# Attention, then two mixtures of experts, on one core: a transpose moved by a chunk, low parts of W1 moved between engines, the second lead's rows turned in one tile

## The chip, the cores and the metric

The kernel runs on one core of a Trainium2 chip. Its time is the device time of one execution in microseconds (us). A profiled execution has in addition a span, from the first to the last instruction that the trace shows. PE is the matmul engine (PEld its weight load), DVE the vector engine, ACT the scalar engine, POOL is GpSimd, and SP issues most DMAs.

## The reference

Three stages follow each other. The first is a linear attention over 2 batches, 8 heads, 768 positions and head size 48, with a decayed state. The second is a mixture of eight experts that gives each of the 1,536 rows to its best expert. The third is such a mixture again, with a capacity for each expert.

```python
# attention, for every position t
cur = einsum(u * k_t, v_t)
y_t = r_t @ (state + cur)
state = w * state + einsum(k_t, v_t)

# first mixture (second: no bias, and rows past an expert's capacity give 0)
logits = x @ w_gate + modality_bias[modality_id]
e_idx = argmax(logits); gate_w = softmax(logits)[e_idx]
for e in range(8):
    h = maximum(x[e_idx == e] @ w1[e], 0.0)      # 384 -> 1024
    out[e_idx == e] = gate_w * (h @ w2[e])       # 1024 -> 384
```

All is float32 outside. Where the kernel wants more than one float32r product gives, it splits a matrix into a high part (a cast) and a low part (the matrix less its cast), and multiplies high by high, low by high and high by low.

## The kernel before, in words

**Attention** goes through 12 chunks of 128 positions (the loop `for i in range(n)`, `n = 12`). In each chunk PE makes the scores (L262), DVE masks them (`am`, L266) and decays keys and queries of the next chunk (L233, L234), PE sums values (L283), and DVE adds POOL's diagonal term `av` (L250) in L288, the chunk's output. POOL's `av` of a chunk needs eight sums that ACT makes (L246), and these need POOL's two products (L240, L241) of the same chunk. Beside the chunks the kernel routes rows for the first mixture: gate logits (L319, L322), a choice (L368 to L376), lists, and from chunk 7 on the expert with most rows is known, the **lead**. Its 256 first rows are gathered to `XB0` (L707) in chunk 10, and its weights are split: `ex.high` on ACT (L677), `ex.low` on DVE or on POOL (L685), in pieces of 128x512, W1 having six.

`ids()` (L1081 to L1084) turns the rows' modality numbers, a 12x128 tile, into a column for each chunk: a DVE cast, a PE transpose, a DVE copy out of PSUM. `biases()` makes the bias of each row from it on POOL (L1088 to L1091), for L322 of chunk 0, which is done in chunk 1 or 2.

**The mixtures.** `Experts.two` does the lead's 256 rows. Its matmuls (L785) are interleaved with the routing of the other rows (hooks by number). Then tiles of 128 rows follow (`tile_a(u)`), each of one expert. A tile is done in a normal form with split weights (`tile1`, L758 up, L806 down), or in a small one (`tile3`, L868, L883, L896). A tile has points at which other work is hooked in: "begin", "first", "turn", "logits", "down", "half", "last". In the run that is profiled the first mixture has tiles 1 to 13; tile 9 is small, tile 10 is normal, tiles 11 to 13 are small. Splitting of the next tile's W1 is in `split1` (L689 a cast on ACT, L690 a subtraction on DVE, in three pieces of 128x1024), and stands under a condition on a number that is read from a table.

For the second mixture a **second lead** is chosen in tile 8 (`PICK`), and its weights are loaded to the same place as the first lead's (`R[0]`, `r0a` and `r0b` in the trace). Its rows are gathered again to `XB0`. From tile 9 on (`SURE - 1`), its rows are turned: `flip` transposes 128 rows on PE (L722, three transposes), and `parts0` makes their high part on ACT (L734) and their low part on DVE (L735). Half 0 is at the "last" point of tile 9, half 1 at that of tile 10. At the "last" point of tile 9 ACT and DVE also read two numbers, `when` and `behind` (`read_when`): in the tile whose number is `when`, ACT and DVE split the second lead's W1. It is 10 in this run. The second `two` starts at 252.08 us.

The order of instructions on each engine is that in which the code is written; nothing is rescheduled. An engine takes its instructions in order and waits at one whose inputs are not there.

Of the kernel before, what the change touches and what calls it, by code (L numbers as in the profile page):

```python
# [18 lines left out]
EN = mybir.EngineType  # L19
# [6 lines left out]
B, H, S, HD = 2, 8, 768, 48  # L26
D = H * HD
# [4 lines left out]
NT = NTOK // P  # L32
# [15 lines left out]
SURE = NTOK // P - 2  # L48
# [541 lines left out]
class Experts:  # L590
# [327 lines left out]

    def read_when(self):

        self.when, self.behind = self.words(3, 2, [EN.Activation, EN.DVE])

    def exit_hint(self, u):

# [115 lines left out]
def program(tc, r, k, v, w, u, mod, wg1, bias, w1a, w2a, wg2, w1b, w2b, cap, out):  # L1040
    nc = tc.nc
    with (
# [9 lines left out]
        banks = [pp.tile([P, 512], F32, name=f"bank{i}") for i in range(8)]  # L1052
# [3 lines left out]
        with tc.tile_pool(name="att", bufs=1) as ap:  # L1056
            ex = Experts(tc, K, wp, mp, banks)
            bs = ap.tile([P, 2, E], F32, name="bs")
            md = ap.tile([NT, P], I64, name="md")
            cpi = ap.tile([P, 1], I64, name="cpi")  # L1060
            wg2s = cp.tile([P, KD, 32], F32, name="wg2s")
            ra = Router(tc, K, mp, banks[7], None, "ra")
            ex.begin(w1a, w2a, x0, x1, ra, wg2s)
            capf = cp.tile([P, 1], F32, name="capf")

            def small():
                nc.sync.dma_start(
                    bs.rearrange("p m e -> p (m e)"),
                    bias.rearrange("m e -> (m e)").unsqueeze(0).to_broadcast([P, 2 * E]),
                )  # L1070
                nc.sync.dma_start(md, mod.rearrange("(c p) -> c p", p=P))

            def small2():
                with nc.allow_non_contiguous_dma(reason="one number a partition"):
                    nc.sync.dma_start(cpi, cap.unsqueeze(0).to_broadcast([P, 1]))
                nc.vector.memset(wg2s, 0.0)
                nc.sync.dma_start(wg2s[:, :, 0:E], wg2.rearrange("(q p) e -> p q e", p=P))

            mdf, mf, b2 = ap.tile([NT, P], F32, name="mdf"), ap.tile([P, NT], F32, name="mf"), ap.tile(TE, F32, name="b2")

            def ids():  # L1081
                nc.vector.tensor_copy(mdf, md.bitcast(I32).rearrange("c (p o) -> c p o", o=2)[:, :, 0])
                nc.tensor.transpose(banks[7][:, 0:NT], mdf, K.ident[0:NT, 0:NT])
                nc.vector.tensor_copy(mf, banks[7][:, 0:NT])  # L1084

            def biases():
                V = nc.gpsimd
                V.tensor_mul(b2, bs[:, 1:2].to_broadcast(TE), mf.unsqueeze(2).to_broadcast(TE))  # L1088
                V.tensor_scalar(mf, mf, -1.0, 1.0, op0=ALU.mult, op1=ALU.add)
                V.tensor_mul(bt, bs[:, 0:1].to_broadcast(TE), mf.unsqueeze(2).to_broadcast(TE))  # L1090
                V.tensor_add(bt, bt, b2)  # L1091

            n = len(ORDER)
            K.begin(nc, ap)
            rows = [xb[:, 0] for xb in ex.XB] + [ex.OB0[:, h] for h in range(2)]
            xts = [ex.xt[:, i] for i in range(2)]
            at = Attention(tc, cp, ap, mp, K, banks, rows, xts, r, k, v, w, u, wg1, bt, x0)
            small()
            for i in range(2, at.NB):
                at.load(i)  # L1100
            small2()
            ex.zero()
            ra.zero()
            at.flip(0)
            at.pnT_()
            at.warm(4)
            at.bonus1(0)
            at.natural_powers()
            at.bonus2()
            at.decayed(0)  # L1110
            for i in range(n):
                more = i + 1 < n
                at.scores(i)
                if more:
                    at.flip(i + 1)
                if i > 0:
                    at.route1(i - 1)
                at.bonus3(i)
                if more:
                    at.bonus1(i + 1)  # L1120
                if more:
                    at.decayed(i + 1)
                if i == 3:
                    nc.gpsimd.tensor_copy(capf, cpi.bitcast(I32)[:, 0:1])
                if i == EARLY + 1:
                    ra.count(0, EARLY)
                if i == EARLY + 4:
                    ra.list0(EARLY)
                    ex.gather(0, ex.XB0, rows=EARLY * P)
                if i == n - 1:  # L1130
                    ex.high(ex.R[0], 5)
                    ex.low(ex.R[0], 4)
                    ex.low(ex.R[0], 1, 3, 5, eng=EN.Pool)
                at.outs(i)
                if i == 0:
                    ids()
                    biases()
                if more:
                    at.bonus2()
                if i > 0:  # L1140
                    at.route2(i - 1)
                if i == EARLY + 4:
                    ex.low(ex.R[0], 0, 2)
                if i + at.NB < n:
                    at.load(i + at.NB)
                if i == EARLY:
                    ra.choose(at.L, 0, EARLY)
                if i == EARLY + 1:
                    ra.lead()
                    ex.load(ex.R[0], w1a, w2a, ra.fe[0:1, 0:1])  # L1150
                    ra.select1(EARLY)
                if i == EARLY + 2:
                    ra.select2(EARLY)
                if i == EARLY + 3:
                    ra.rows(EARLY)
                    ex.high(ex.R[0], 0, 2, 4)
                if i == EARLY + 4:
                    ra.spent(EARLY)
                    ex.high(ex.R[0], 1, 3)
                if i == 2:  # L1160
                    K.more(nc, cp)
                if i == 3:
                    K.more2(nc, cp)
            px = [banks[2][:, 0:D], banks[3][:, 0:D]]
            for h in range(2):
                ex.flip(ex.XB0, h, px[h])
            for h in range(2):
                ex.parts0(h, px[h])
            at.route1(n - 1)
        with tc.tile_pool(name="moeb", bufs=1) as mb:  # L1170
# [103 lines left out]
            def tile_a(u):  # L1274

                H = {p: [] for p in ("begin", "first", "turn", "logits", "down", "half", "last")}
# [31 lines left out]

                if u == PICK:
                    H["last"].insert(0, b3)  # L1310
                if u in (SURE - 1, SURE):
                    h = u - SURE + 1
                    H["last"] += [lambda: ex.flip(ex.XB0, h), lambda: ex.parts0(h)]
                if u == SURE - 1:
                    H["last"].append(ex.read_when)
                H["down3"] = [(lambda p: lambda: part2(p))(p) for p in range(2) if u > SURE + p]
# [5 lines left out]
                def split1():  # L1322
                    if u < U:
                        with tc.If(ex.split(u + 1)):
                            ex.split1(ex.slot(u + 1))
                    if u >= SURE:
                        with tc.If(ex.when == u):
                            ex.split1(ex.R[0])

                nothing = lambda: None  # L1330
                nxt = (
                    (lambda: ex.flip(xb(u + 1))) if u < U else nothing,
                    ex.parts if u < U else nothing,
                    split1,
                )
                if SURE <= u < U:
# [22 lines left out]
            def tile_b(u):  # L1359
# [16 lines left out]
                {-1: [a0, a1], 0: [a2], 2: [a3], 8: [ra.plan2], 10: [a4], 18: [ex.read, first_tile], 22: [ra.early]}  # L1376
            )
            tile_a(1)

            ex.begin(w1b, w2b, x1, out, rb)  # L1380
# [48 lines left out]
```

## Time and profile before

| | us |
|---|---|
| median of 3 runs | 377.67 |
| lowest, highest | 376.71, 382.09 |
| the profiled execution | 377.47 |
| its span in the trace | 375.8 |
| outside of the span | 1.7 |

PE is busy for 330.5 us of the span, DVE for 232.0, ACT for 156.0, POOL for 134.8. The matmul clock granted is 0.961 of the full one on average. Attention fills the span up to about 75 us, the first `two` from there to about 97 us, tiles 1 to 8 to 194 us, tile 9 to 205 us, tile 10 to 222 us, tiles 11 to 13 to 249 us, and the second mixture the rest.

### The profile page before, as it was taken

What the parts mean: (1) busy time and instruction counts of PE and PEld (TensorE: products, weight loads), DVE (VectorE), ACT (ScalarE), POOL (GpSimd) and SP (SyncE); (2) the same over time, 40 slices, a digit from 0 to 9 for tenths busy, and PEclk for the clock granted to TensorE, in tenths of its full rate; (3) what the DMA queues carried; (4) which work ended last, traced back from release to release, by engine and by line L of the source; (5) the groups of instructions that cost most, each with busy time, mean ns of one, the idle gap of its engine ahead of it and who ended that gap; (6) DMA issues with size and microseconds to landing.
All of it is one profiled execution on the core that took longest, in us unless ns stands there. A gap on an engine that the chain in (4) does not pass through costs nothing. (4 is left out here: it accounts for less than half of the span.)

```text
span 375.8 us, 9045 instructions
## 1 busy us (share of the span) xinstructions
PE 330.5 (88%) x2888; PEld 271.1 (72%) x2888; DVE 232.0 (62%) x675; ACT 156.0 (42%) x500; POOL 134.8 (36%) x165
## 2 busy tenths in 40 slices
PE   7699999969999999999995969869997989998960
PEld 6699988859878888888873844449886877574430
DVE  5679899979853444444657776645838395753330
ACT  3577566725042233333215644423146263823220
POOL 7888876935503222111214222311522212232230
PEclk9899999958999999999999898999999999999995
DMA  7858679452262111029899990000189998999400
GB/s 141 152 121 182 151 159 330 156 210 91 59 231 96 46 44 34 34 60 371 323 406 394 335 334 24 11 19 3 44 298 390 340 346 294 391 347 393 161 14 13
DMA packets 69509, 70.94 MB, mean 189 GB/s; under 512 B 41542, under 2 KB 61744, under 8 KB 69416
## 3 DMA queue, kind: packets, MB, share of 16 engines
q1 hardware_dynamic: 65704, 61.69, 50.0%
q0 software_dynamic: 3712, 8.18, 6.6%
q8 instruction: 38, 0.62, 0.7%
q14 instruction: 55, 0.45, 0.4%
HBM read 60.73 MB, written 12.55 MB: 195 GB/s over the span
## 5 line engine op out<-in xcount | busy, mean ns | idle before, releaser
L714 POOL DMA_INDIRECT x<-ob,raidx x14 | 15.3, 1095 | 104.8 <-DVE sn L845 57.9
L774 DVE TENSOR_TENSOR hl<-bank,hh 128x512 fp32r<-128x512 f32 x28 | 19.1, 689 | 39.8 <-ACT hh L773 38.5
L763 ACT ACTIVATE hs<-bank 128x512 f32<-128x512 f32 x28 | 16.7, 598 | 54.7 <-PE bank L758 46.7
L758 PE MATMUL bank<-w1l,xh 128*128 128x512 f32 x84 | 34.1, 407 | 3.3 <-DVE g L747 3.1
L714 POOL DMA_INDIRECT out<-ob,rbidx x12 | 12.1, 1006 | 69.2 <-DVE ex L742 57.1
L806 PE MATMUL bank<-w2h,hh 128*128 128x384 f32 x144 | 35.0, 353 | 0.0
L758 PE MATMUL bank<-w1h,xh 128*128 128x512 f32 x84 | 34.1, 407 | 0.0
L758 PE MATMUL bank<-w1h,xl 128*128 128x512 f32 x84 | 33.9, 403 | 0.0
L806 PE MATMUL bank<-w2l,hh 128*128 128x384 f32 x144 | 33.2, 337 | 0.1
L806 PE MATMUL bank<-w2h,hl 128*128 128x384 f32 x144 | 32.5, 335 | 0.0
L806 PEld LDWEIGHTS bank<-w2h,hh 128*128 128x128 f32 x144 | 24.2, 188 | 2.3 <-issue 2.0
L806 PEld LDWEIGHTS bank<-w2l,hh 128*128 128x128 f32 x144 | 25.6, 188 | 0.4 <-POOL w2l L685 0.4
L806 PEld LDWEIGHTS bank<-w2h,hl 128*128 128x128 f32 x144 | 25.6, 188 | 0.0
L246 ACT ACTIVATE rk<-rk 128x48 f32<-128x48 f32 x96 | 21.8, 230 | 3.8 <-POOL rk L241 3.8
L758 PEld LDWEIGHTS bank<-w1l,xh 128*128 128x128 f32 x84 | 16.2, 192 | 8.1 <-DVE g L747 3.9
L707 POOL DMA_INDIRECT xb<-x,raidx x17 | 19.2, 1131 | 7.3 <-issue 3.9
L707 POOL DMA_INDIRECT xb<-x,rbidx x14 | 17.1, 1218 | 11.1 <-ACT hs L886 6.2
L812 DVE TENSOR_SCALAR ob<-bank,g 128x384 f32<-128x384 f32 x18 | 11.1, 618 | 15.1 <-PE bank L806 13.8
L758 PEld LDWEIGHTS bank<-w1h,xh 128*128 128x128 f32 x84 | 16.2, 193 | 4.1 <-ACT w1h L689 0.6
L758 PEld LDWEIGHTS bank<-w1h,xl 128*128 128x128 f32 x84 | 16.1, 191 | 3.8
L722 PE MATMUL bank<-ident,xb 128*128 128x128 f32 x87 | 14.2, 274 | 4.8 <-DVE ob L903 3.7
L785 PE MATMUL bank<-xh,w1h 128*128 128x256 f32 x48 | 15.6, 325 | 3.1 <-DVE ex L742 3.0
(310 smaller groups left out, 827.8 us busy)
## 6 DMA issues: line engine op xcount, KB each, us to landing
r1a<-in_moe_w SPq DMA_DIRECT2D x5, 1536.0 KB
r1b<-in_moe_w SPq DMA_DIRECT2D x5, 1536.0 KB, 8.8
r3a<-in_moe_w SPq DMA_DIRECT2D x4, 1536.0 KB, 7.8
r3b<-in_moe_w SPq DMA_DIRECT2D x4, 1536.0 KB
r2a<-in_moe_w SPq DMA_DIRECT2D x4, 1536.0 KB, 7.8
r2b<-in_moe_w SPq DMA_DIRECT2D x4, 1536.0 KB, 11.4
r0a<-in_moe_w SPq DMA_DIRECT2D x2, 1536.0 KB, 10.5
r0b<-in_moe_w SPq DMA_DIRECT2D x2, 1536.0 KB
```

The source lines that it names most:

```text
L246: self.nc.scalar.activation(self.rk[:, h], self.rk[:, h], AF.Copy, accum_out=self.a[:, h : h + 1])
L707: self.nc.gpsimd.indirect_dma_start(out=xb[:, h], out_offset=None, in_=x[0:rows], in_offset=bass.IndirectOffsetOnAxis(ap=idx[:, j + h : j ...
L714: return self.nc.gpsimd.indirect_dma_start(out=out, out_offset=bass.IndirectOffsetOnAxis(ap=idx[:, j : j + 1], axis=0), in_=ob, in_offset= ...
L722: self.nc.tensor.transpose(px[:, q * P : (q + 1) * P], xb[:, h, q * P : (q + 1) * P], self.K.ident)
L758: self.nc.tensor.matmul(self.banks[n], lhsT=a[:, 0, q], rhs=b[:, f : f + 512], start=(i == 0), stop=(i == 8))
L763: self.nc.scalar.activation(self.HS[n], self.banks[n], AF.Relu)
L774: self.nc.vector.tensor_tensor(self.hl[:, s, 0], pt, self.hh[:, s, 0].bitcast(F32), op=ALU.subtract)
L785: self.nc.tensor.matmul(ps, lhsT=w[:, s], rhs=x[:, :, q], start=(i == 0), stop=(i == 8))
L806: self.nc.tensor.matmul(self.po[h], lhsT=a[:, m, h], rhs=b[:, m * D : (m + 1) * D], start=(m == 0 and k == 0), stop=(m == KF - 1 and k == 2),)
L812: self.nc.vector.tensor_scalar(ob[:, h, 0:D], self.po[h], self.g[2][:, h : h + 1], None, op0=ALU.mult)
```

## The change

There are four parts.

**A.** `ids()` is cut in two. The DVE cast stays behind `outs(0)`. The PE transpose moves to chunk 1, behind `flip(2)`, and the copy out of PSUM goes to ACT. `biases()` goes to chunk 1, behind `bonus3(1)`, which is POOL's `av`.

**B.** One of six low parts of the first lead's W1 (piece 4) moves on DVE from chunk 11 to chunk 10, beside pieces 0 and 2.

**C.** Both halves of the second lead's rows are turned at the "logits" point of tile 10, into banks 73 and 74 of the trace, and no longer at the "last" points of tiles 9 and 10.

**D.** The second lead's W1 is split in six pieces: the high parts on ACT (L677), the low parts on POOL (L685) in place of DVE. POOL reads `when` too and has the branch.

```diff
     def read_when(self):
-        self.when, self.behind = self.words(3, 2, [EN.Activation, EN.DVE])
+        self.when, self.behind = self.words(3, 2, [EN.Activation, EN.DVE, EN.Pool])
...
-            def ids():
+            def ids1():
                 nc.vector.tensor_copy(mdf, md.bitcast(I32).rearrange("c (p o) -> c p o", o=2)[:, :, 0])
+
+            def ids2():
                 nc.tensor.transpose(banks[7][:, 0:NT], mdf, K.ident[0:NT, 0:NT])
-                nc.vector.tensor_copy(mf, banks[7][:, 0:NT])
+                nc.scalar.copy(mf, banks[7][:, 0:NT])
...
                 at.scores(i)
                 if more:
                     at.flip(i + 1)
+                if i == 1:
+                    ids2()
                 if i > 0:
                     at.route1(i - 1)
                 at.bonus3(i)
+                if i == 1:
+                    biases()
...
                 if i == n - 1:
                     ex.high(ex.R[0], 5)
-                    ex.low(ex.R[0], 4)
                     ex.low(ex.R[0], 1, 3, 5, eng=EN.Pool)
                 at.outs(i)
                 if i == 0:
-                    ids()
-                    biases()
+                    ids1()
...
                 if i == EARLY + 4:
-                    ex.low(ex.R[0], 0, 2)
+                    ex.low(ex.R[0], 0, 2, 4)
...
-                if u in (SURE - 1, SURE):
-                    h = u - SURE + 1
-                    H["last"] += [lambda: ex.flip(ex.XB0, h), lambda: ex.parts0(h)]
+                if u == SURE:
+                    p0, p1 = (banks[h][:, 0:D] for h in range(2))
+                    H["logits"] += [lambda: ex.flip(ex.XB0, 0, p0), lambda: ex.flip(ex.XB0, 1, p1)]
+                    H["logits"] += [lambda: ex.parts0(0, p0), lambda: ex.parts0(1, p1)]
...
                     if u >= SURE:
                         with tc.If(ex.when == u):
-                            ex.split1(ex.R[0])
+                            ex.high(ex.R[0], *range(6))
+                            ex.low(ex.R[0], *range(6), eng=EN.Pool)
```

On PE, chunks 0 and 1: the transpose of the modality numbers (`mdf`) stood between the last state sums of chunk 0 (L296) and the scores of chunk 1 (L262).

```order
 L283 MATMUL bank_77<-vt_157,am 64x48 x16
 L296 MATMUL bank_78<-vt_157,kn 48x48 x8
-L1083 MATMUL bank_80<-ident,mdf 128x12
 L262 MATMUL bank_75<-rb_180,kb_182 128x128
 L262 MATMUL bank_76<-rb_180,kb_182 128x128
```

It now stands after the two groups L232 of the next `flip`, as L1085; the scores of chunk 1 are next to L296.

On POOL in the same chunks: the four instructions of `biases` (`bt` and `b` are the biases, `mf` the modality numbers) and `av` of chunk 1 (L250).

```order
 L256 TENSOR_TENSOR kn<-kt_154,pn 128x384
-L1088 TENSOR_TENSOR b_119<-bs,mf 128x96
-L1089 TENSOR_SCALAR mf<-mf 128x12
-L1090 TENSOR_TENSOR bt<-bs,mf 128x96
-L1091 TENSOR_TENSOR bt<-bt,b_119 128x96
 L250 TENSOR_TENSOR av<-vt_158,a 128x384
+L1090 TENSOR_TENSOR b_119<-bs,mf 128x96
+L1091 TENSOR_SCALAR mf<-mf 128x12
+L1092 TENSOR_TENSOR bt<-bs,mf 128x96
+L1093 TENSOR_TENSOR bt<-bt,b_119 128x96
 L240 TENSOR_TENSOR rk<-rt_151,kt_155 128x384
```

They have moved from ahead of `av` to behind it, ahead of the products of the next chunk (L240).

On DVE, chunks 10 and 11: the low parts of the first lead's W1 (L685) around the masks of chunk 11 (L266).

```order
 L322 TENSOR_TENSOR L<-bank_79,bt 128x8
-L685 TENSOR_TENSOR w1l<-r0a,w1h 128x512 x2
+L685 TENSOR_TENSOR w1l<-r0a,w1h 128x512 x3
 L266 TENSOR_TENSOR am<-bank_75,mask 128x512
 L266 TENSOR_TENSOR am<-bank_76,mask 128x512
-L685 TENSOR_TENSOR w1l<-r0a,w1h 128x512
 L288 TENSOR_TENSOR xb_96<-bank_77,av 128x384
```

The third low part is now ahead of the masks, and the output of chunk 11 (L288) follows the masks at once.

On POOL, tile 10, from its start to the first instruction of the next tile's routing (L714 is a scatter of finished rows). Before:

```order
L926 ISA
L1425 BRANCH_PREFETCH_HINT
L1324 UNCONDITIONAL_BRANCH
L1327 UNCONDITIONAL_BRANCH
L714 DMA x_72<-ob_98,raidx 1536x392
L474 TENSOR_SCALAR rac_1328<-racs 128x8
```

And now:

```order
L926 ISA
L1431 BRANCH_PREFETCH_HINT
L1329 UNCONDITIONAL_BRANCH
L1332 COMPARE_AND_BRANCH
L685 TENSOR_TENSOR w1l<-r0a,w1h 128x512 x6
L1332 UNCONDITIONAL_BRANCH x2
L714 DMA x_72<-ob_98,raidx 1536x392
L474 TENSOR_SCALAR rac_1329<-racs 128x8
```

Six subtractions now stand ahead of the scatter and of L474, a step of the second mixture's routing.

## Rows read from the trace of the kernel before

**Rows 1.** Waits of PE: who waited for whom, us in total, times, longest.
```profile
PE bank L722 <- DVE ob L903: 3.7, 1, 3.7
...
PE bank L309 <- DVE L L322: 3.1, 1, 3.1
...
PE bank L1083 <- DVE mdf L1082: 3.0, 1, 3.0
```

**Rows 2.** Stretches: length, busy time (instructions) by engine, granted clock, DMA share, GB/s.
```profile
45.00:70.00 25.00, 23.46 (x465) 22.02 (x462) 23.75 (x58) 18.79 (x113) 18.51 (x19) 1.00 0.82 231
76.60:86.90 10.30, 8.63 (x53) 7.80 (x54) 7.29 (x27) 4.71 (x12) 2.72 (x7) 0.50 0.76 272
106.00:201.50 95.50, 93.96 (x628) 79.66 (x626) 46.52 (x172) 33.23 (x86) 19.40 (x20) 1.00 0.50 177
```

**Rows 3.** Timeline, PE, chunk 1: start, duration, instruction, idle before it.
```profile
15.59 2.08 PE L262 MATMUL bank<-rb,kb 64*128 64x128 f32 x16
```

**Rows 4.** Timeline, POOL, chunks 1, 2 and 6.
```profile
16.09 0.35 POOL L1088 TENSOR_TENSOR b<-bs,mf 128x96 f32<-128x96 f32 x1
...
17.59 0.83 POOL L250 TENSOR_TENSOR av<-vt,a 128x384 f32<-128x384 f32 x1
...
22.96 0.83 POOL L250 TENSOR_TENSOR av<-vt,a 128x384 f32<-128x384 f32 x1 [1.52 <-ACT rk L246]
...
43.08 0.83 POOL L250 TENSOR_TENSOR av<-vt,a 128x384 f32<-128x384 f32 x1 [1.05 <-ACT ob L323]
```

**Rows 5.** Timeline, DVE, the output of chunk 6.
```profile
45.92 0.56 DVE L288 TENSOR_TENSOR xb<-bank,av 128x384 f32<-128x384 f32 x1
```

**Rows 6.** Timeline, DVE and one instruction of PE, chunks 10 and 11.
```profile
70.69 1.28 DVE L685 TENSOR_TENSOR w1l<-r0a,w1h 128x512 fp32r<-128x512 f32 x2
71.89 1.28 DVE L266 TENSOR_TENSOR am<-bank,mask 128x512 f32<-128x512 f32 x2
73.08 4.41 DVE L685 TENSOR_TENSOR w1l<-r0a,w1h 128x512 fp32r<-128x512 f32 x1
77.42 0.55 DVE L288 TENSOR_TENSOR xb<-bank,av 128x384 f32<-128x384 f32 x1
...
72.63 1.27 PE L283 MATMUL bank<-vt,am 128*64 128x48 f32 x32 [0.30 <-DVE am L266]
```

**Rows 7.** Timeline, POOL, chunks 10 and 11.
```profile
72.28 0.21 POOL L474 TENSOR_SCALAR rac<-racs 128x8 f32<-128x8 f32 x1
...
73.24 3.70 POOL L685 TENSOR_TENSOR w1l<-r0a,w1h 128x512 fp32r<-128x512 f32 x3
```

**Rows 8.** Timeline, several engines, tiles 9 to 11.
```profile
200.57 3.50 DVE L690 TENSOR_TENSOR w1l<-r1a,w1h 128x1024 fp32r<-128x1024 f32 x3
...
205.49 0.52 PE L722 MATMUL bank<-ident,xb 128*128 128x128 f32 x3 [3.69 <-DVE ob L903]
...
206.56 0.56 DVE L735 TENSOR_TENSOR xl<-bank,xh 128x384 fp32r<-128x384 f32 x1 [1.18 <-ACT xh L734]
...
216.13 2.95 ACT L689 CAST w1h<-r0a 128x1024 fp32r<-128x1024 f32 x3 [1.43 <-DVEq L1324]
217.21 3.56 DVE L690 TENSOR_TENSOR w1l<-r0a,w1h 128x1024 fp32r<-128x1024 f32 x3 [1.31 <-ACT w1h L689]
219.51 1.02 POOL L714 DMA_INDIRECT x<-ob,raidx  x1 [10.21 <-ACT racs L473]
...
220.87 0.15 DVE L748 TENSOR_SCALAR g<-g 128x1 f32<-128x1 f32 x1
...
222.75 0.32 POOL L484 TENSOR_TENSOR raeqc<-raeqc,low 128x64 f32<-128x64 f32 x1 [1.92 <-DVE raeqc L482]
...
224.62 0.56 DVE L875 TENSOR_SCALAR hs<-bank 128x384 f32<-128x384 f32 x1 [0.26 <-issue]
```

**Rows 9.** Timeline, the first `two`: a small DVE instruction beside POOL's low parts.
```profile
87.33 1.22 DVE L748 TENSOR_SCALAR g<-g 128x2 f32<-128x2 f32 x1
...
85.55 2.96 POOL L685 TENSOR_TENSOR w2l<-r0b,w2h 128x512 fp32r<-128x512 f32 x2 [4.00 <-ACT w2h L677]
```

## The prediction, made before the changed kernel ran

> **What bounds the kernel now.** I read the waits of PE first, since PE is by far the busiest engine. Three of its longest waits, of 3.7, 3.1 and 3.0 us, stand at the places that the change touches [rows 1]: PE waits ahead of tile 10, in chunk 11 for the logits behind L288, and in chunk 1 for the cast of the modality numbers, whose transpose L1083 stands ahead of the scores. Next come the stretches. From 106 to 201.5 us PE is busy for 93.96 of 95.5 us [rows 2], so what is gained before it arrives whole at tile 9. From 45 to 70 us DVE is busy for 23.75 of 25 us, more than PE [rows 2]: there a gain of PE alone is worth little. Then the timelines around each place, for who holds whom.
>
> **Part A, the ids.** PE waited 3.0 us [rows 1], and the scores behind it start at 15.59 [rows 3]. Without the transpose there they can start some 3 us earlier. Added is a small ACT copy of 0.2 us, in place of the DVE copy; nothing there waits for it but the biases. What is paid: the biases held POOL from 16.09 to 17.59, 1.5 us [rows 4], mostly while `av` would have waited for ACT's sums anyway. Now they stand behind `av` and ahead of the two products (L240, L241) that ACT's next sums need. The next `av` (22.96) had 1.52 us of waiting for ACT ahead of it [rows 4], so part of the 1.5 is hidden there; I take 0.6 us, between 0 and 1.5. DVE's L288 of a chunk needs its `av`. In chunk 6 `av` starts at 43.08 and takes 0.83 [rows 4], and L288 starts at 45.92 [rows 5]: 2.0 us to spare. If POOL is 0.6 later, at most 1.4 us of PE's 3 pass this point. Behind it DVE is the full engine, and I take **-1.0 us**. Bounds: -3.0, if POOL and ACT follow, as their waits for each other are not at their limit, and +0.6, if POOL sets the pace all along.
>
> **Part B, one low part on DVE.** In chunk 10 two low parts took 1.28 us together, in chunk 11 the third took 4.41, from 73.08 to 77.49 [rows 6]. It began beside POOL, whose three low parts run from 73.24 to 76.94 without a gap [rows 7], and it ended 0.55 us behind them, about its own length of 0.64: it stood still until POOL's whole run of three was over. Behind it in DVE's queue is L288, the output of chunk 11 (77.42), and PE waits 3.1 us for the logits that follow from it [rows 1]. Now the piece goes ahead of the masks, as the third of a row: 0.64 us added to L266 (71.89), which starts near 72.5, and L283 on PE with it. That instruction begins on the first mask and takes 1.27 us [rows 6], so L288 runs near 72.5 + 0.64 + 1.27 = 74.4 or a little later: 2.9 us earlier. The routing behind it moves along. PE ran at a granted clock of 0.50, the lower of its two levels (1.2 of 2.4 GHz), from 76.6 to 86.9 us, behind its wait [rows 2]; I count 0.5 us for what it gets back, since the routing on DVE and POOL, not PE, ends that stretch. I take **-3.4 us**, with bounds of -2.3 (POOL's three low parts hold another DVE instruction with two operands in SBUF for a part of the time) and -4.8 (8.63 us of PE at half the clock are 4.3 at the full one, and a third of that passes on).
>
> **Parts C and D, tile 10.** They meet and are costed together. Removed: PE's wait of 3.69 us ahead of the transposes of `XB0` [rows 8]. Late next are the low parts of tile 10's own W1, which DVE ends at 204.07 (200.57 + 3.50) [rows 8]; the up-projection can begin on the first of the three at 201.8, so about 3 us of the 3.7 is real. Added at the "logits" point: six transposes on PE, 1.0 us (two rows of 0.52), and two instructions like L735, of 0.56 us [rows 8], on each of ACT and DVE, ahead of the next tile's parts: 1.1 us. ACT's casts of the second lead's W1, at 216.13 [rows 8], thus start near 214.2. The casts themselves cost the same, six halves for three wholes. DVE loses 3.56 us of low parts. POOL gains six of 3.70 / 3 = 1.23 us [rows 7], 7.4 us, from about 214.9 (a half cast later) to 222.3. No one needs them before 252 us. But two things stand behind them. On POOL's queue these are the scatter L714 (1.02 us) and the routing steps L474 and L484; DVE waits for the latter. On DVE it is the small L748 (220.87 before, 0.15 us [rows 8]): beside two of POOL's low parts the same line took 1.22 us and ended as they did (88.55 and 88.51) [rows 9]. So it will stand until 222.3. From L748 to L875, which makes tile 11's activations, it was 3.75 us [rows 8]; less L735, which has gone (0.5), that gives 222.3 + 3.75 - 0.5 = 225.55 for L875, against 224.62. I take **+0.9 us**: what the front gave is spent, and 0.9 more. PE waits for L875 longer instead. The low end is -2.0: the front's 3 us less the 1.1 added, if POOL holds nobody. The high end is +3.0: if the front doesn't move, POOL's run starts 2 us later. The words that POOL now reads cost it about a microsecond, in a stretch in which it waits for 10.21 us [rows 8]: nothing, and if POOL were full, 1 us.
>
> POOL's run of three beside a held DVE decides C and D as it does B. The Trainium skill, in "SBUF — State Buffer", section "Who interferes with whom", has a rule that differs from these rows: the pair of ports that the two engines share is locked for a whole instruction and the other "fully blocks", so that DVE should come in between two of POOL's. The row of 4.41 us speaks against it, as it spans three.
>
> If DVE came in between, L748 would be through by 219.5, and only POOL's own queue would be late: L484 comes at 222.3 + 1.0 + 0.3 = 223.6 instead of 222.75 [rows 8], and less the 0.5 of L735, L875 is 0.3 later than it was instead of 0.9. The sum would be 0.6 lower.
>
> **The sum.** The profiled execution took 377.47 us (375.8 of span and 1.7 around it); the median of the three is 377.67, 0.2 above it. 377.47 - 1.0 - 3.4 + 0.9 = 373.97; in terms of the median I say **374.2 us**. The rest of the program is unchanged: the stages behind 226 us start earlier by as much and depend on nothing that stays.
>
> **Rivals.**
> 1. *More is gained.* POOL and ACT follow PE in part A, so its -3.0 lasts, or L748 isn't held and tile 10's front is kept. For: in part A POOL itself waits for ACT, which waits for PE. Against: DVE at 95% from 45 to 70 us, and POOL's run of 7.4 us. 377.47 - 3.0 - 3.4 + 0.9 = 372.0; with tile 10's -2.0 in place of +0.9 it is 377.47 - 1.0 - 3.4 - 2.0 = 371.1; about 369.1 with both.
> 2. *Slower: the third low part loses the race in chunk 10.* It now starts at about 71.9 (where L266 did), and POOL's next instructions are L474 at 72.28 and `av` at 72.45, with the three low parts behind [rows 6, 7]. It decides whether DVE's third piece begins before 72.28, a margin of 0.4 us. If not, DVE stands from there to 76.9 ahead of the masks of chunk 11 rather than behind them: masks at 77.5 (76.94 and the piece's own 0.6) instead of 71.89, which leaves L288 near 79.5, 2.1 us later than now. 377.47 - 1.0 + 2.1 + 0.9 = 379.5. Against: part A makes DVE earlier and POOL later.
> 3. *It does little.* POOL sets the pace in part A (+0.6), B gives 2.3, and tile 10 costs 2.0, which is possible as its run of low parts ends on the path: 377.47 + 0.6 - 2.3 + 2.0 = 377.8.
>
> **Chances.** The forecast (372.6 to 376.2) 0.57, the first rival 0.19, the third 0.16, the second 0.08. The range of 370.4 to 378.2 leaves out the second rival, the far end of the first, and the upper end of the third, together under 0.2. A difference of under 2% can't be told from none by these runs: faster by more is below 370.1, slower above 385.2. Only the far end of the first rival lies below: 0.06. Above 385.2 lies none of the cases: 0.01 for what I haven't seen. Within 2%: 0.93.
>
> **What the profile of the changed kernel will show.** For A: the scores L262 of chunk 1 near 12.5 us and 1.2 us long, and L288 of chunk 6 near 44.5 to 45. For B: three L685 of DVE in one row of 1.9 us, none of 4 us, L288 of chunk 11 near 73.5 to 74.5, and no wait of 3 us ahead of L309. For C and D: no wait of 3.7 us ahead of tile 10, six L685 of POOL in a run of 7.4 us, L748 lasting until its end, and PE's wait for L875 longer than before. I'm wrong on tile 10 if L748 takes 0.15 us there and L875 comes earlier relative to the tile's start than it did. I'm wrong on B if L266 of chunk 11 is later than 74.

## The result and the profile after

The changed kernel takes 372.56 us (median of 4 runs, 371.4 to 373.4) against 377.19 for the kernel before: a ratio of 0.9874, 95% interval 0.9827 to 0.9921. In a second set of runs it was 0.9884 (0.9842 to 0.9926). The profiled execution took 373.11 us, with a span of 371.3. The forecast was 374.2: the gain is 4.6 us instead of 3.5. The whole interval lies below 1; the gain is clear, but under 2%. The range held, but the terms were not those that I had written down. Ratios compare the runs that lie within 1.5% of the fastest of their kernel; of the version called "ACT and POOL later" below, three of six runs lay above that.

PE's waits of the changed kernel (who waited for whom, us in total, times, longest), answering to [rows 1]:

```profile
PE bank L883 <- DVE hs L875: 10.2, 4, 7.5
PE bank L785 <- DVEq L1358: 3.6, 1, 3.6
...
PE bank L1085 <- DVE mdf L1082: 0.5, 1, 0.5
```

The three waits of [rows 1] have gone: 0.5 us is left of the one for the ids, and L722 and L309 wait for nothing long. A wait of 7.5 us has come ahead of L883 in tile 11, where it was 3.2 us before. The 3.6 us at the branch into the second mixture were 3.1 before.

PE in chunk 1, POOL and DVE in chunk 6 (start, duration, instruction, idle before it), answering to [rows 3 to 5]:

```profile
12.55 1.16 PE L262 MATMUL bank<-rb,kb 64*128 64x128 f32 x16
...
43.56 0.83 POOL L250 TENSOR_TENSOR av<-vt,a 128x384 f32<-128x384 f32 x1 [1.05 <-ACT ob L323]
...
44.42 0.56 DVE L288 TENSOR_TENSOR xb<-bank,av 128x384 f32<-128x384 f32 x1 [0.59 <-POOL av L250]
```

The scores of chunk 1 are 3.0 us earlier, POOL's `av` of chunk 6 is 0.5 us later, and DVE's L288 is 1.5 us earlier.

DVE, then POOL, in chunks 10 and 11, answering to [rows 6, 7]:

```profile
68.92 1.88 DVE L685 TENSOR_TENSOR w1l<-r0a,w1h 128x512 fp32r<-128x512 f32 x3
70.73 1.28 DVE L266 TENSOR_TENSOR am<-bank,mask 128x512 f32<-128x512 f32 x2
72.84 0.56 DVE L288 TENSOR_TENSOR xb<-bank,av 128x384 f32<-128x384 f32 x1 [0.83 <-issue]
...
71.63 3.72 POOL L685 TENSOR_TENSOR w1l<-r0a,w1h 128x512 fp32r<-128x512 f32 x3
```

The three low parts of DVE take 1.88 us together, 0.63 each; none is held. L288 of chunk 11 is 4.6 us earlier. DVE was already 1.8 us earlier where the low parts begin (68.92 against 70.69).

Tile 10 and 11 on several engines, answering to [rows 8]:

```profile
196.26 0.48 PE L758 MATMUL bank<-w1h,xh 128*128 128x512 f32 x1
...
203.92 0.88 PE L722 MATMUL bank<-ident,xb 128*128 128x128 f32 x6
...
208.38 3.22 ACT L677 CAST w1h<-r0a 128x512 fp32r<-128x512 f32 x6 [2.63 <-DVEq L1329]
...
209.09 7.41 POOL L685 TENSOR_TENSOR w1l<-r0a,w1h 128x512 fp32r<-128x512 f32 x6 [4.87 <-ACT w1h L677]
216.64 1.03 POOL L714 DMA_INDIRECT x<-ob,raidx  x1
217.70 0.21 POOL L474 TENSOR_SCALAR rac<-racs 128x8 f32<-128x8 f32 x1
217.87 0.32 POOL L484 TENSOR_TENSOR raeqc<-raeqc,low 128x64 f32<-128x64 f32 x1
...
211.74 0.16 DVE L747 TENSOR_REDUCE g<-ex 128x1 f32<-128x8 f32 x1 [3.50 <-ACT ex L746]
211.94 0.15 DVE L748 TENSOR_SCALAR g<-g 128x1 f32<-128x1 f32 x1
...
212.84 1.24 DVE L849 TENSOR_SCALAR rv<-cm,sn 128x12 bf16<-128x12 bf16 x1
214.00 0.60 DVE L812 TENSOR_SCALAR ob<-bank,g 128x384 f32<-128x384 f32 x1
214.53 0.83 DVE L482 TENSOR_TENSOR raeqc<-rasofar 128x64 f32<-128x64 f32 x1
215.28 1.30 DVE L483 TENSOR_TENSOR ralow<-rasofar 128x64 f32<-128x64 f32 x1
218.22 0.22 DVE L485 TENSOR_TENSOR ralow<-ralow,raeqc 128x64 f32<-128x64 f32 x1 [1.64 <-POOL raeqc L484]
...
219.28 0.56 DVE L875 TENSOR_SCALAR hs<-bank 128x384 f32<-128x384 f32 x1 [0.26 <-issue]
...
219.89 0.90 PE L883 MATMUL bank<-ident,hs 128*128 128x128 f32 x3 [7.54 <-DVE hs L875]
```

Tile 10 starts right behind tile 9, 9.6 us earlier than before. Then all of that is lost: POOL's six low parts run from 209.09 to 216.50 without a gap, the scatter and the routing steps L474 and L484 come behind them, L485 on DVE waits for L484, and L875 stands at 219.28, which is 5.34 us earlier than before and no more than L875 of tile 9 was (5.39). DVE's chain to L875 starts with L747, which waits 3.50 us for the softmax on ACT (L746), behind the six casts; L747 is still 9.0 us earlier than before (220.69), so the loss lies behind it.

### The profile page after: what moved, and what is told of

Same layout as the page of the kernel before. It is cut to its first block, busy times and chain, and to the rows that moved or that the text cites. A ratio compares the mean times of both kernels' runs of the same rounds, so it can differ in the third digit from the quotient of the medians.

```text
span 371.3 us, 9065 instructions
## 1 busy us (share of the span) xinstructions
PE 326.4 (88%) x2888; PEld 267.5 (72%) x2888; DVE 225.1 (61%) x671; ACT 155.7 (42%) x504; POOL 141.1 (38%) x171
## 5 line engine op out<-in xcount | busy, mean ns | idle before, releaser
L714 POOL DMA_INDIRECT x<-ob,raidx x14 | 15.7, 1124 | 96.0 <-DVE sn L845 74.8
L714 POOL DMA_INDIRECT out<-ob,rbidx x12 | 11.9, 994 | 66.3 <-DVE ex L742 55.9
L758 PE MATMUL bank<-w1l,xh 128*128 128x512 f32 x84 | 33.8, 402 | 3.4 <-DVE g L747 2.9
L758 PE MATMUL bank<-w1h,xh 128*128 128x512 f32 x84 | 33.6, 399 | 0.0
L758 PE MATMUL bank<-w1h,xl 128*128 128x512 f32 x84 | 33.2, 395 | 0.0
L758 PEld LDWEIGHTS bank<-w1l,xh 128*128 128x128 f32 x84 | 15.7, 187 | 8.9 <-DVE g L747 3.7
L707 POOL DMA_INDIRECT xb<-x,raidx x17 | 18.2, 1068 | 7.1 <-issue 2.8
L812 DVE TENSOR_SCALAR ob<-bank,g 128x384 f32<-128x384 f32 x18 | 11.1, 617 | 14.9 <-PE bank L806 13.6
L785 PE MATMUL bank<-xh,w1h 128*128 128x256 f32 x48 | 15.0, 312 | 4.0 <-DVEq L1358 3.6
L758 PEld LDWEIGHTS bank<-w1h,xh 128*128 128x128 f32 x84 | 15.8, 188 | 3.8 <-ACT w1h L689 0.6
L758 PEld LDWEIGHTS bank<-w1h,xl 128*128 128x128 f32 x84 | 15.8, 188 | 3.5
L246 ACT ACTIVATION_READ_ACCUMULATOR rk<-rk 128x1 f32 x96 | 18.0, 187 | 0.0
## 6 DMA issues: line engine op xcount, KB each, us to landing
r0a<-in_moe_w SPq DMA_DIRECT2D x2, 1536.0 KB, 10.3
```

Source lines behind the costliest of these rows:

```text
L246: self.nc.scalar.activation(self.rk[:, h], self.rk[:, h], AF.Copy, accum_out=self.a[:, h : h + 1])
L707: self.nc.gpsimd.indirect_dma_start(out=xb[:, h], out_offset=None, in_=x[0:rows], in_offset=bass.IndirectOffsetOnAxis(ap=idx[:, j + h : j ...
L714: return self.nc.gpsimd.indirect_dma_start(out=out, out_offset=bass.IndirectOffsetOnAxis(ap=idx[:, j : j + 1], axis=0), in_=ob, in_offset= ...
L758: self.nc.tensor.matmul(self.banks[n], lhsT=a[:, 0, q], rhs=b[:, f : f + 512], start=(i == 0), stop=(i == 8))
L785: self.nc.tensor.matmul(ps, lhsT=w[:, s], rhs=x[:, :, q], start=(i == 0), stop=(i == 8))
L812: self.nc.vector.tensor_scalar(ob[:, h, 0:D], self.po[h], self.g[2][:, h : h + 1], None, op0=ALU.mult)
```

## The experiments

The table gives, for each kernel's profile, how far five instructions stand from their place in the profile before (its start less the start before; negative is earlier): L288 of chunk 10 (68.96 us before), the first L758 of tile 1 (103.21), the first L758 of tile 10 (205.88), L875 of tile 11 (224.62) and the first L785 of the second mixture (252.08). The last column is the time's ratio to the kernel before in the same set of runs, with its interval. The places are all held against the one profile of the kernel before, whichever chip and set a run was in. The kernel before has medians of 377.2 to 380.8 us in the four sets of runs, so times are compared as ratios.

| kernel | chunk 10 | tile 1 | tile 10 | tile 11 | second | ratio |
|---|---|---|---|---|---|---|
| changed | -2.9 | -5.7 | -9.6 | -5.3 | -4.2 | 0.987 (0.983 to 0.992) |
| changed, again | -2.7 | -5.3 | -9.2 | -4.8 | -3.6 | 0.988 (0.984 to 0.993) |
| A undone | +1.5 | -1.8 | -5.9 | -1.5 | +0.2 | 1.000 (0.995 to 1.005) |
| B undone | -2.9 | -5.8 | -9.7 | -5.4 | -4.0 | 0.998 (0.993 to 1.003) |
| B undone, again | -2.9 | -5.3 | -9.1 | -4.8 | -2.9 | 0.991 (0.985 to 0.997) |
| A and B undone | +0.5 | +0.5 | -3.7 | +0.5 | +1.9 | 1.006 (1.002 to 1.010) |
| C undone | -2.8 | -5.9 | -5.6 | -2.9 | -0.7 | 0.999 (0.995 to 1.003) |
| one low part on DVE | -2.9 | -5.3 | -9.2 | -5.7 | -5.2 | one run |
| all low parts on DVE | -2.7 | -5.3 | -9.1 | -8.0 | -7.2 | 0.978 (0.971 to 0.985) |
| ACT and POOL later | -2.6 | -6.2 | -10.1 | -11.4 | -10.3 | 0.974 (0.966 to 0.982) |
| A and B only | -2.8 | -5.4 | -4.8 | -4.3 | -4.7 | 0.981 (0.974 to 0.988) |

Up to tile 10 the two kernels that were profiled twice repeat within 0.6 us, but kernels of the same code up to tile 1 lie there between -5.3 and -6.2, so a place is good to about a microsecond. Behind tile 13 the same kernel scatters by some microseconds, so up to there the columns say more than the ratio.

**A undone.**

```diff
-                if i == 1:
-                    ids2()
...
-                if i == 1:
-                    biases()
...
                 if i == 0:
-                    ids1()
+                    ids()
+                    biases()
```

> The changed kernel with part A undone (transpose, copy and biases of the modality numbers behind chunk 0 as before). Theory: A is worth about 1.8 us, the part of its 3 us that still stood at the low parts of chunk 10 (70.69 before, 68.92 in the changed kernel), and B is worth what it was without it: the wait of 3 us for the cast is back, L288 of chunk 10 runs near 69 instead of 66.1, tile 1 begins 1.8 us later than in the changed kernel, the time is about 374.4 us. Rival: POOL and the lists set the pace in chunks 7 to 11 whatever PE does, A is worth nothing by then, tile 1 begins within 0.5 us of the changed kernel, 372.6 us.

Tile 1 begins 4.0 us later than in the changed kernel, and by the ratio the whole gain is gone. Of the 4.0 us, 1.4 are PE's clock: behind the same wait as before PE stayed at the lower clock level longer in this run (from 18.5 to 20.3 us the granted clock is 0.50, and 0.97 in the kernel before). PE in chunk 1 of it:

```profile
15.41 0.25 PE L1083 MATMUL bank<-ident,mdf 12*128 12x12 f32 x1 [2.97 <-DVE mdf L1082]
...
20.00 1.72 PE L275 MATMUL bank<-st,rb 128*128 128x96 f32 x8
```

L275 of this chunk took 1.03 us in the kernel before and 1.72 here. The theory had A too small (1.8); the rival (nothing) is out.

**B undone.**

```diff
                 if i == n - 1:
+                    ex.low(ex.R[0], 4)
                     ex.low(ex.R[0], 1, 3, 5, eng=EN.Pool)
...
-                    ex.low(ex.R[0], 0, 2, 4)
+                    ex.low(ex.R[0], 0, 2)
```

> The changed kernel with part B undone (low part 4 behind the masks of chunk 11). Theory: DVE's low part stands until POOL's whole run of three is over: about 4.2 us long, PE waits 3 us for the logits of chunk 11 and falls to half the clock, tile 1 begins 3.5 to 4 us later than in the changed kernel, about 376.4 us. Rival (the ports are taken for one instruction at a time): DVE comes in after POOL's first low part, its own takes at most 1.9 us, PE's wait is under 1 us, tile 1 about 1 us later, 373.6 us.

The theory fell. DVE's piece in chunk 11, and POOL's run beside it:

```profile
71.34 1.47 DVE L685 TENSOR_TENSOR w1l<-r0a,w1h 128x512 fp32r<-128x512 f32 x1
...
70.99 4.18 POOL L685 TENSOR_TENSOR w1l<-r0a,w1h 128x512 fp32r<-128x512 f32 x3
```

DVE came in after POOL's first piece, and POOL's run is 0.5 us longer for it. Tile 1 begins as early as in the changed kernel: with A in place, B is worth nothing up to there. The ratio of this kernel was nevertheless that of the kernel before, so I ran it once more.

> The changed kernel with part B undone, a second time. Its ten times lay in two groups, 375 us (two of them, one the profiled) and 378 us and more. Theory: in the slower group DVE's low part stands through POOL's whole run of three as in the kernel before, 4.4 us, and tile 1 begins 3 to 4 us later; with A in place the piece is at the edge of being held. If this profile is of the slower group it shows a piece of over 4 us; if of the faster one, 1.5 us again. Rival: the groups come from the second mixture, and the piece takes 1.5 us in a slow run too.

This profile is of a run of 377.94 us, where the shortest took 373.48, and the piece took 1.42 us in it. So the rival holds for the piece. Against the first profile of this kernel (a run of 374.96 us, on another chip) 0.6 us is lost by tile 1, 1.1 by the start of the second mixture, and 3.3 by an L758 in it (295.85 against 292.54): most of the spread lies behind the start of the second mixture. Whether B has a worth in the median is not settled by these two ratios.

**A and B undone.** Both edits above together.

> The changed kernel with A and B both undone (C and D kept). Theory (A or B alone is enough to get DVE's low part out of POOL's run): with both gone the piece takes over 4 us again, PE waits 3 us in chunk 11, and tile 1 begins within 0.5 us of the kernel before or up to 1.4 us later, as the clock was low for longer in the run with A undone; against the run with A undone, tile 1 is 3 us later. Rival: the 4.41 us were a chance of that one run, the piece takes under 2 us here, and tile 1 begins as with A undone alone. Time 377 to 380 us by the theory, against 375 to 377 by the rival.

```profile
73.55 4.41 DVE L685 TENSOR_TENSOR w1l<-r0a,w1h 128x512 fp32r<-128x512 f32 x1
...
73.69 3.71 POOL L685 TENSOR_TENSOR w1l<-r0a,w1h 128x512 fp32r<-128x512 f32 x3
```

The 4.41 us of [rows 6] are back to the hundredth, and tile 1 is where it was in the kernel before. The rival (a chance of one run) is out. With A undone alone, B takes 3.2 us out between chunk 10 and tile 1 (+1.5 to -1.8); with neither, nothing is taken out (+0.5 to +0.5). So either part alone frees the piece, and their gains don't add. The ratio, 1.006, is that of C and D alone: they give nothing without A and B.

**C undone.** The two turns back at the ends of tiles 9 and 10.

```diff
-                if u == SURE:
...
+                if u in (SURE - 1, SURE):
+                    h = u - SURE + 1
+                    H["last"] += [lambda: ex.flip(ex.XB0, h), lambda: ex.parts0(h)]
```

> The changed kernel with part C undone (the second lead's rows turned at the ends of tiles 9 and 10, D kept). Theory: PE's wait of about 3.7 us ahead of tile 10 is back, ACT's casts and POOL's run of six low parts start 3 us later or more, and since POOL's scatter and routing step behind that run set L875 of tile 11, L875 and all after it come 3 us later: about 375.5 us. Rival: L875 is set by something that doesn't hang on the front of tile 10 (DVE's chain from the softmax on), and it moves by less than 1 us: 373 us.

```profile
199.85 0.52 PE L722 MATMUL bank<-ident,xb 128*128 128x128 f32 x3 [3.63 <-DVE ob L903]
...
211.03 7.45 POOL L685 TENSOR_TENSOR w1l<-r0a,w1h 128x512 fp32r<-128x512 f32 x6 [7.31 <-ACT w1h L677]
...
219.87 0.33 POOL L484 TENSOR_TENSOR raeqc<-raeqc,low 128x64 f32<-128x64 f32 x1
...
221.75 0.56 DVE L875 TENSOR_SCALAR hs<-bank 128x384 f32<-128x384 f32 x1 [0.26 <-issue]
```

The direction of the theory, at less than its 3 us: the wait is back, POOL's run starts 1.9 us later, and L875 comes 2.5 us later (1.9 against the second profile of the changed kernel), 0.5 of it from an L735 that stands ahead of it again. So with D in place, C is worth 1.9 to 2.5 us at L875. The second mixture begins 3.5 us later, and the ratio is 1.2% higher, about 4.5 us; what is lost behind tile 11 is not explained.

**One low part on DVE, five on POOL.**

```diff
-                            ex.low(ex.R[0], *range(6), eng=EN.Pool)
+                            ex.low(ex.R[0], *range(5), eng=EN.Pool)
+                            ex.low(ex.R[0], 5)
```

> The changed kernel with one of the six low parts in tile 10 given to DVE, five left on POOL; DVE's piece becomes ready while POOL's run is on. Theory (DVE stands until POOL's run is over, as in chunk 11 of the kernel before): DVE's piece lasts to the end of POOL's fifth, 3 to 4.5 us. Rival (one instruction at a time): it takes at most 1.23 + 0.64 = 1.9 us, and POOL's run has a gap or a longer piece there. In both cases POOL's queue is 1.2 us earlier; L875 of tile 11 moves by -1.2 by the rival and by -1 to 0 by the theory; time 372 to 373 us.

```profile
212.02 1.76 DVE L685 TENSOR_TENSOR w1l<-r0a,w1h 128x512 fp32r<-128x512 f32 x1 [3.39 <-ACT w1h L677]
...
209.47 6.68 POOL L685 TENSOR_TENSOR w1l<-r0a,w1h 128x512 fp32r<-128x512 f32 x5 [4.88 <-ACT w1h L677]
...
217.54 0.32 POOL L484 TENSOR_TENSOR raeqc<-raeqc,low 128x64 f32<-128x64 f32 x1
...
218.96 0.56 DVE L875 TENSOR_SCALAR hs<-bank 128x384 f32<-128x384 f32 x1 [0.26 <-issue]
```

For the piece the rival is right: DVE waited for one piece of POOL's (1.76 less its own 0.63). POOL's queue was not 1.2 us earlier, as both had it: five pieces and DVE's turn took 6.68 us, 0.5 us more than five pieces alone. L484 came 0.33 us earlier than in the first profile of the changed kernel and L875 0.32; against the second, 0.86 and 0.85.

**All six low parts on DVE** (C kept).

```diff
-                            ex.low(ex.R[0], *range(6), eng=EN.Pool)
+                            ex.low(ex.R[0], *range(6))
```

> The changed kernel with the six low parts in tile 10 on DVE (C kept, D without POOL). Theory: DVE takes 6 x 0.6 = 3.8 us for them, as fast as ACT casts, POOL's queue is empty, L875 of tile 11 comes near 216 instead of 219.3, 3 us earlier than in the changed kernel: D costs 3 us. Rival (DVE's own work is what sets L875, as D supposes): L875 no earlier than in the changed kernel, 0 to +1 us.

```profile
209.51 3.73 DVE L685 TENSOR_TENSOR w1l<-r0a,w1h 128x512 fp32r<-128x512 f32 x6 [0.79 <-ACT w1h L677]
...
215.22 0.32 POOL L484 TENSOR_TENSOR raeqc<-raeqc,low 128x64 f32<-128x64 f32 x1 [1.44 <-DVE raeqc L482]
...
216.63 0.56 DVE L875 TENSOR_SCALAR hs<-bank 128x384 f32<-128x384 f32 x1 [0.26 <-issue]
```

The theory held to 0.6 us. The six pieces take DVE 3.73 us, half of what they take POOL, and now POOL waits for DVE. L875 is 2.7 us earlier than in the changed kernel, 3.2 against its second profile: giving this work to POOL cost that much.

**ACT's casts and POOL's low parts later in tile 10.** They move to the tile's "last" point: ACT's casts behind the softmax (L746), POOL's low parts behind the scatter and L484.

```diff
                     if u >= SURE:
-                        with tc.If(ex.when == u):
-                            ex.high(ex.R[0], *range(6))
-                            ex.low(ex.R[0], *range(6), eng=EN.Pool)
...
+                def second():
+                    with tc.If(ex.when == u):
+                        ex.high(ex.R[0], *range(6))
+                        ex.low(ex.R[0], *range(6), eng=EN.Pool)
+
+                if u >= SURE:
+                    H["last"].append(second)
```

> The changed kernel with the second lead's W1 split later in tile 10: ACT's six casts and POOL's six low parts stand behind the next tile's softmax input on ACT and behind the scatter and the routing step on POOL. Theory (POOL's queue and ACT's casts ahead of the softmax set L875 of tile 11, where the gain of the front was lost): L875 comes near 212 instead of 219.3, 7 us earlier than in the changed kernel, PE's wait of 7.5 us ahead of L883 shrinks to under 1, and the second mixture begins 4 to 7 us earlier, since POOL's run now lies beside tile 11 and can hold single instructions of DVE there by up to 1.2 us each. Time 4 to 7 us under that of the changed kernel on the same chip. Rival (something behind, the branch out of tile 13 or the loads, gives the time back): L875 earlier but the time within 2 us of the changed kernel's.

```profile
207.91 0.16 DVE L747 TENSOR_REDUCE g<-ex 128x1 f32<-128x8 f32 x1
...
210.45 0.32 POOL L484 TENSOR_TENSOR raeqc<-raeqc,low 128x64 f32<-128x64 f32 x1 [0.81 <-DVE raeqc L482]
210.73 7.44 POOL L685 TENSOR_TENSOR w1l<-r0a,w1h 128x512 fp32r<-128x512 f32 x6
...
210.81 1.28 DVE L485 TENSOR_TENSOR ralow<-ralow,raeqc 128x64 f32<-128x64 f32 x1 [0.30 <-POOL raeqc L484]
...
213.18 0.55 DVE L875 TENSOR_SCALAR hs<-bank 128x384 f32<-128x384 f32 x1
...
213.78 0.55 PE L883 MATMUL bank<-ident,hs 128*128 128x128 f32 x3 [1.46 <-DVE hs L875]
```

L875 is 6.1 us earlier than in the changed kernel, the second mixture begins 6.1 us earlier, and PE waits 1.5 us ahead of L883 in place of 7.5. Not all of it is POOL's queue, since two things have moved: with the softmax ahead of ACT's casts L747 starts 3.8 us earlier (207.91 against 211.74), and with POOL's run behind L484 the rest follows. No run moves one of them alone. The ratio, 0.974, is the lowest of all; the changed kernel on the same chip has 0.988, and all low parts on DVE 0.978, with an interval that overlaps this one.

**The changed kernel again**, on that chip:

> The changed kernel once more, on the same chip as the others of this set. Theory: up to tile 10 the milestones repeat to 0.3 us, and what differs from run to run lies behind it, at branches. It is 3 to 5 us faster than the kernel before. Rival: the gain of 4.6 us of the first measurement was in part chance behind tile 10 (the profile shows 3 us of the gain in the last tiles), and here it is 2 us or less.

The ratio repeats, and the rival is out; the places up to tile 10 repeat to 0.2 to 0.5 us. What doesn't repeat is the profile of the second mixture's tiles: from their first L875 (318.59 us before) to the last (358.81) the first profile gained 2.9 us, this one 0.5. As it is from another set of runs than the profile before, the chip and the kernel can't be told apart there.

**A and B only** (tile 10 as it was):

> The kernel before with A and B alone (tile 10 as it was). Theory: C's 3 to 5 us and D's loss cancel at tile 11, so L875 of tile 11 comes as early as in the changed kernel (219.3 in its trace, within 0.4 us), and the branch out of tile 13, which now finds POOL's program as it was, costs what it cost before, 2 us less than in the changed kernel: the second mixture begins 2 us earlier than there, and the ratio to the kernel before is 0.982 to 0.988. Rival: C and D give 1 us or more net, L875 comes later by that, and the ratio is 0.990 or above.

L875 of tile 11 is 0.5 to 1.0 us later than in the two profiles of the changed kernel, the second mixture begins 0.5 to 1.1 us earlier. So C and D together give nothing up to there. Of the 1.0 us by which the first profile of the changed kernel leads at L875 of tile 11, nothing is left at L875 of tile 12 (-4.65, here -4.76): PE's long wait there is followed by 3 us at a granted clock of 0.50, here by 1.00. Another 0.4 us goes at the branch. The theory was wrong on the size of that: the wait at the branch is 3.27 us here, but the 3.3 us behind it run at 0.51 as in the changed kernel. The ratio lies in the range of the theory and outside the rival's; its interval overlaps that of the changed kernel.

## Why the prediction was right, and where it was not

**Part A was mis-sized**: -1.0 us in the sum, -2.9 at chunk 10. Its step on POOL held: POOL was to be 0.6 us later, and its `av` is 0.5 to 0.6 later in chunks 2 and 6; 1.4 us were to pass chunk 6, and L288 there is 1.5 us earlier. The step behind it, "behind it DVE is the full engine", failed. DVE was full, but partly of standing still. Three small instructions of the kernel before between 54 and 61 us, and the same three of the changed kernel:

```profile
54.06 0.97 DVE L428 TENSOR_TENSOR rasel<-raoh,ras 128x48 f32<-128x48 bf16 x1
...
59.34 0.98 DVE L442 TENSOR_SCALAR ramm<-rark 128x6 f32<-128x6 f32 x1
...
60.44 0.97 DVE L444 SCALAR_TENSOR_TENSOR rari<-ramm,rark 128x6 f32<-128x6 f32 x1
```

```profile
52.80 0.21 DVE L428 TENSOR_TENSOR rasel<-raoh,ras 128x48 f32<-128x48 bf16 x1
...
57.32 0.17 DVE L442 TENSOR_SCALAR ramm<-rark 128x6 f32<-128x6 f32 x1
...
57.60 0.16 DVE L444 SCALAR_TENSOR_TENSOR rari<-ramm,rark 128x6 f32<-128x6 f32 x1
```

In the kernel before each begins 0.05 to 0.1 us behind an instruction of POOL's (L240 at 53.96 and 59.29, L241 at 60.37) and ends within 0.1 us of it. With DVE earlier against POOL they fall between POOL's instructions: 0.97 to 0.98 us become 0.16 to 0.21, 2.4 us together. From chunk 7 to chunk 9, L288's lead grows from 1.2 to 3.2 us. POOL did not follow meanwhile, as the first rival had it: its `av` of chunk 8 is still 0.2 us later than before. The three are short in all nine profiles with part A and long in the three without it. No run moves DVE against POOL alone, so this account of A is read from the rows and not shown by an experiment. A busy time on DVE of 95% [rows 2] is no proof of work.

**Part B was right in mechanism and size, but not as a term to be added.** Alone it gives 3.2 us (forecast 3.4); beside A it gives none up to tile 1, since with A the piece begins inside POOL's run and is held for one of POOL's instructions only. A and B together gave 5.3 to 6.2 us at tile 1, where the sum had 4.4.

**Parts C and D**: +0.9 in the sum; at L875 they came to +0.05 in the first profile (-5.39 at tile 9, -5.34 at tile 11), then 0.7 more by L875 of tile 12 (234.08 before, 4.65 us earlier now), since PE ran part of tile 11 at the lower of its two clock levels behind its wait of 7.5 us (a granted clock of 0.50 from 219.9 to 222.9 us). The front gave more than the 3 us taken: from L875 of tile 9 to the start of tile 10 the lead grows by 4.2, the whole wait and the transposes. The wrong step is the one on L748: it was to stand until POOL's run ended, and took 0.15 us. The row that it rested on didn't bear it out: there L748 has another form (128x2), and it begins at 87.33, when the second of POOL's two pieces has just begun (87.22), so it was held for one [rows 9]. L849, L482 and L483 were held, none longer than one piece of POOL's run. What set L875 was the other half of that part, POOL's own queue (L484 behind six pieces and a scatter), as L485's wait of 1.64 us shows: L875 stands 1.41 or 1.42 us behind L484 in the changed kernel, in its repeat, and with one or all low parts on DVE. So the alternative beside the sum (DVE comes in between, +0.3) was right. The forecast's own sign of being wrong on tile 10 was half met: L748 took 0.15 us, but L875 came later against the tile's start (23.0 us behind it, 18.7 before). At L875, C without POOL is worth 3.7 us (all low parts on DVE against A and B only), and D takes 2.7 to 3.2 of it.

**Left out of the forecast: the branch out of tile 13.** "The rest of the program is unchanged" was wrong for it. PE's first matmul of the second mixture, in the kernel before and in the changed one:

```profile
252.08 0.36 PE L785 MATMUL bank<-xh,w1h 128*128 128x256 f32 x1 [3.05 <-DVE ex L742]
```

```profile
247.88 0.53 PE L785 MATMUL bank<-xh,w1h 128*128 128x256 f32 x1 [3.64 <-DVEq L1358]
```

and the stretch of 3.3 us from there (length, busy by engine, granted clock, DMA), before and after:

```profile
252.10:255.40 3.30, 3.30 (x29) 2.98 (x30) 0.43 (x2) 0.64 (x2) 0.00 (x0) 1.00 0.03 5
```

```profile
247.90:251.20 3.30, 3.30 (x15) 3.30 (x16) 0.77 (x4) 0.34 (x1) 0.24 (x2) 0.50 0.03 10
```

PE waits 0.6 us longer for DVE to come back from the branch, and then runs 3.3 us at half clock, which costs 1.5. From tile 13 (-4.78 at its L875) to the 18th of these matmuls the lead falls to 2.65 us.

The wait is 2.99 to 3.27 us in the four profiles in which DVE has low parts in tile 10's branch (the kernel before, A and B only, one or all low parts on DVE), and 3.64 to 4.72 us in the eight in which it has none. POOL's additional branch alone is therefore not what makes it long, as it is there too with one low part on DVE (2.99 us). Why DVE comes late is open. The half clock doesn't go with this wait: in the first 3.3 us behind it the granted clock is 1.00 in the kernel before and with all low parts on DVE, and 0.50 to 0.70 in the ten others.

**Part of the near hit is luck.** In the first profile the lead was 5.3 us at tile 11 and 2.65 us behind the branch, where the sum had 3.5 throughout. At the end of the span it was 4.5: the second mixture's tiles gave 2.9 us, and some of that was lost again at the very end. This late gain did not repeat: the second profile of the changed kernel has a span only 0.7 us shorter than the kernel before (375.1 against 375.8), which was profiled in another set. The ratio of the medians did repeat. So more from A and B, a loss at the branch and a late gain made up a total near the forecast. By the ratios the gain is that of A and B (0.981 with them alone, 1.006 without them); how it comes through the second mixture is not shown.

## What to carry to other kernels

An instruction given to an idle engine must be put behind that engine's short steps that others wait for: POOL's 7.4 us ahead of a routing step cost 2.7 to 3.2 us at L875, and with POOL's run and ACT's casts both behind such steps L875 came 6.1 us earlier. Two edits that free the same instruction don't add up, so cost them together, and undo each of them and both. Before a busy engine is called the bound, look whether its small instructions have their usual length.

## What the runs showed of the hardware

DVE instructions beside a run of POOL subtractions were mostly held for one POOL instruction at most: 1.47, 1.42 and 1.76 us for a piece of 0.63, and 1.24 to 1.30 us for small ones. The Trainium skill, "SBUF — State Buffer", section "Who interferes with whom", states that the pair of ports which the two engines share goes to one of them for a whole instruction, while the other is blocked, and that a DVE instruction with two inputs in SBUF is concerned. These rows agree with the lock for one instruction. In two profiles, the kernel before and A and B undone, the piece nevertheless stood for all three of POOL's (4.41 us, twice). In both it began while POOL's `av` was running, and the run followed at once; in the other three it began inside the run. Why it was passed over three times is open.

The form seems to matter too: L748 on 128x1 took 0.15 us inside POOL's run in all nine profiles in which POOL has low parts in tile 10, and on 128x2 1.22 us in the one row that there is [rows 9]. L812, whose big input lies in PSUM, kept its 0.60.
